# Early Q and K loads, and one 64-column selection turn for chunks 1 to 3, in a fused windowed-attention and maxout-FFN kernel

## The chip, the cores and the metric

The kernel runs on one core of one Trainium2 chip. The metric is device time in microseconds (us), from start to end of one execution. Kernels that were run together ran on the same chip and shared runs of the kernel before. A ratio is the mean time of one kernel's fast runs over that of the other's of the same rounds, with a 95% interval, so it isn't quite the ratio of the medians that are quoted beside it. Four runs count as slow (one of e4, three of the kernel before in sets B and C); the ratios leave them out, the quoted medians and ranges hold them. The experiments ran in three sets on three chips (set A: e1, e2, e4, e5; set B: e6, e8, e9, e10; set C: e3, e11, e12, e13). Between sets I compare ratios to the kernel before, not times.

## The reference, cut to what matters

```python
# attention: q, k, v are (4, 8, 768, 64): 4 batches, 8 heads, 768 tokens, 64 per head
scores = (1 / np.sqrt(D)) * np.matmul(q, k.transpose(0, 1, 3, 2))
keep = (pos[None, :] < 4) | ((rel >= 0) & (rel < 128))        # 4 sink tokens, window of 128
a = softmax(np.where(keep, scores, -1e9))
x = np.matmul(a, v)  # heads side by side: 3072 tokens x 512
# maxout FFN: w1, w2, w3 are 512 x 768, w_out is 768 x 512
h = np.maximum(np.maximum(x @ w1, x @ w2), x @ w3)
out = (h @ w_out).astype(np.float32)
```

## The kernel before

The tokens are worked through in 12 chunks of 256, three to a batch. For each chunk Q and K are loaded and turned (head dimension onto partitions), the scores are made, exponentials taken, multiplied with V ("AV"), the result is turned and goes into the FFN. All instructions are placed by hand: every engine works its own list in order, so an instruction that waits holds up all later ones of its engine (in e12 below a cast starts 5.9 us after its data have landed). In the order string, `K`, `Q` are turns, `B` the mask bias in PSUM, `S` scores, `A` AV, `T` the turn of the result, `F` a group of the FFN; the letter after it names the chunk (`a` is chunk 0, `b` is chunk 1 in the start).

Two kinds of loads exist. Chunk 0 goes through SyncE's queue in fp32 and is cast on VectorE; chunks 1 and 2 go through Pool's queue in runs of 16 tokens and are converted to bf16 by the load:

```python
def load_runs(ci):
    ...
    for j, src in ((0, k), (1, q)):
        nc.gpsimd.dma_start(
            out=runs[ci][:, j],
            in_=src[b, :, t0:t0 + 256].rearrange("h (r x) d -> h r (x d)", x=16))
```

Runs are turned by matmuls with columns of the identity. Chunk 1 uses 64 columns of the data at a time; chunk 2 uses 128, which takes half as many matmuls but leaves each head's data on the wrong half of the partitions for half of it, so that the copies out of PSUM are 64 partitions by 256:

```python
def prep_runs(ci, j, g):
    ...
    if ci == 1:
        for i in range(2):
            pt = psum.tile([128, 8, NP, 16], F32, tag="f", name="pt")
            for u in range(8):
                for h in range(2):
                    nc.tensor.matmul(pt[64 * h:64 * h + 64, u],
                                     lhsT=x[:, 128 * u + 64 * i:128 * u + 64 * i + 64],
                                     rhs=heads[:, h], start=True, stop=True)
            ...                                    # one wide copy out, L258 or L260
        return
    pt = psum.tile([128, 8, 4, 16], F32, tag="f", name="pt")
    for u in range(8):
        nc.tensor.matmul(pt[:, u], lhsT=x[:, 128 * u:128 * u + 128],
                         rhs=ident[:, 64 * g:64 * g + 64], start=True, stop=True)   # L264
    ...                                            # four narrow copies out, L271 or L273
```

Chunk 3 is loaded in fp32 and cast on Pool. The start:

```python
load(0)                                  # SyncE queue: K, Q, K, Q of chunk 0, then its V
...                                      # Pool: identity, four selects, masks, sel, v_sink
sink_v_init()
load_runs(1)                             # Pool queue, its first loads
load_v(1, nc.gpsimd)
load_w(0, 0, 256)
load_w(0, 256, d_ff)
warm(36)                                 # filler matmuls that keep TensorE's clock up
...
run("Ka1 Sa01 Qa1 Ba23", a=0)
run("Sa23", a=0)
cast_v(0, 0, nc.vector)
cast_v(0, 1, nc.vector)
nc.gpsimd.tensor_copy(v_sink[:, :, 0:D], vs_raw)
sink_k(0, nc.gpsimd.tensor_copy)
load_w(1, 0, 256)
load_w(1, 256, d_ff)
load_w(2)
...
warm(3)
run("Aa0 Aa1 Aa2 Aa3 Kb0 Qb0 Ta0 Ta1 Bb01 Sb01 Zb", a=0, b=1)
```

The softmax here doesn't subtract the row's maximum and nothing guards it: scores larger than these inputs give would overflow.

## Time and profile before

| kernel before | |
|---|---|
| time | 184.04 us median of 3 runs, 182.4 to 184.81 |
| span in the profile | 181.6 us |
| TensorE busy | 94% of the span |
| bytes read, written | 25.2 MB, 6.29 MB |

The prediction below shows the busy row, the chain and the stretches. The page's slices: 40 equal parts of the span, each digit a share in tenths (9 is 90% or more). These are the clock that TensorE was granted, and the busy share of the DMA engines:

```profile
PEclk9999999999999999999999999999999999999999
DMA  4999999899598989991589989898799742132404
```

The clock is at its full rate throughout, and the DMA engines are busy for 80% or more of slices 2 to 10, the first 45 us. The order of time in the first 30 us (start, duration, engine, line, operation, output<-input, shapes, count, and in brackets the idle time before it and what ended it):

```profile
5.55 0.94 POOL L84 DMA_DIRECT2D runs<-in_k_dram  x1
...
6.84 0.51 DVE L203 CAST qk_bf<-qk_raw 128x512 bf16<-128x512 f32 x1 [0.26 <-DMA qk_raw<-in_q_dram]
...
8.61 2.18 DVE L212 CAST ve<-v_raw 64x512 bf16<-64x512 f32 x4 [0.34 <-DMA v_raw<-in_v_dram]
...
10.84 0.80 PE L374 MATMUL o_ps<-ve,e_sb 128*128 128x65 bf16 x21 [0.73 <-DVE ve L212]
...
10.89 2.23 POOL L162 DMA_DIRECT2D w<-in_moe_w_dram  x3
...
13.16 0.70 PE L253 MATMUL pt<-ident,runs 128*64 128x64 bf16 x32 [0.89 <-DMA runs<-in_q_dram]
```

Pool's first load is issued at 5.55 us, and when it begins to move, at 7.38 (see below), nearly all of chunk 0 is in: its last piece of Q is cast at 6.84, its V at 8.61 as it lands, and AV of chunk 0 starts in earnest at 10.84 (three matmuls of it at 9.84), before chunk 1's runs are turned. Below, the start of AV is always that of its main part.

### The profile page before, as it was taken

Reading aid. Unit: us, or ns where it says so; the run is one execution under the profiler, and the core shown is the slowest. Engines: PE = TensorE matmul, PEld = TensorE weight load, DVE = VectorE, ACT = ScalarE, POOL = GpSimd, SP = SyncE. Lnnn points to the kernel's source line nnn. Section 1 sums busy time; section 2 is a strip of 40 time slices with the busy share of each in tenths; the row PEclk is TensorE's granted clock in tenths of the full one; section 3 lists DMA queues with packets and bytes.
Section 4 is the critical chain, followed back from the end, with each engine's and each line's share of the span. In section 5 each row is a group of like instructions: output and inputs, shape, how many; then the busy total and the mean of one; then the engine's idle time right before and its main releaser. Section 6 shows DMA issues by size and latency. Waiting matters only on the chain.

```text
span 181.6 us, 4832 instructions
## 1 busy us (share of the span) xinstructions
PE 170.8 (94%) x1953; PEld 131.6 (72%) x1953; DVE 118.4 (65%) x251; ACT 92.1 (51%) x197; POOL 70.7 (39%) x121
## 2 busy tenths in 40 slices
PE   6949999979999999999999899999999999999991
PEld 6645789755698688588598488687696796796880
DVE  1785435997299189577667767676695785673451
ACT  2537651962881781951933922923826716622220
POOL 7986700657621565565014623626244400000001
PEclk9999999999999999999999999999999999999999
DMA  4999999899598989991589989898799742132404
GB/s 142 236 182 204 209 206 249 191 288 289 144 187 207 255 209 302 228 296 64 105 221 306 161 239 270 152 269 229 159 298 198 135 106 58 34 85 58 119 2 116
DMA packets 64646, 33.64 MB, mean 185 GB/s; under 512 B 26640, under 2 KB 60944, under 8 KB 64624
## 3 DMA queue, kind: packets, MB, share of 16 engines
q1 hardware_dynamic: 59520, 27.70, 64.1%
q0 software_dynamic: 4864, 5.38, 16.4%
q8 instruction: 15, 0.25, 0.6%
q10 hardware_dynamic: 240, 0.26, 0.6%
q14 instruction: 7, 0.06, 0.1%
HBM read 25.20 MB, written 6.29 MB: 173 GB/s over the span
## 4 chain that ended last, share of the span: by engine, by line
PE 76%; DMA 11%; DVE 3%; SPq 2%; ACT 2%; issue 1%; POOL 1%; POOLq 0%
PE h_ps L412 49%; PE y_ps L433 15%; DMA w<-in_moe_w_dram 7%; PE o_ps L374 5%; PE st L322 3%; DMA xT<-x_sb 2%; DMA vs_raw<-in_v_dram 2%; DVE h_sb L418 2%; PE y_ps L452 1%; SPq L70 1%; SPq L110 1%; ACT e_sb L328 1%; DVE kk L273 1%; PE o_ps L361 1%; PE sk L341 1%
## 5 line engine op out<-in xcount | busy, mean ns | idle before, releaser
L412 PE MATMUL h_ps<-xT,w 128*128 128x256 bf16 x864 | 103.5, 273 | 1.2 <-DMA xT<-x_sb 0.6
L412 PEld LDWEIGHTS <-w 128*128 128x128 bf16 x864 | 81.3, 98 | 13.2 <-issue 1.4
L418 DVE TENSOR_TENSOR h_sb<-h_sb,h_ps 128x512 bf16<-128x512 bf16 x72 | 49.1, 684 | 27.0 <-PE h_ps L412 22.3
L328 ACT ACTIVATE e_sb<-st 128x512 bf16<-128x512 f32 (+1 forms) x96 | 45.2, 594 | 5.5 <-PE st L322 5.4
L416 ACT CAST h_sb<-h_ps 128x512 bf16<-128x512 f32 x36 | 21.8, 611 | 46.8 <-PE h_ps L412 46.7
L212 POOL CAST ve<-v_raw 64x512 bf16<-64x512 f32 x44 | 31.2, 709 | 27.3 <-DMA v_raw<-in_v_dram 22.0
L203 POOL CAST qk_bf<-qk_raw 128x512 bf16<-128x512 f32 x36 | 22.8, 635 | 44.5 <-DMA qk_raw<-in_k_dram 27.6
L335 DVE TENSOR_TENSOR e_sb<-e_sb,msk 128x1024 bf16<-128x1024 bf16 (+1 forms) x40 | 29.1, 741 | 16.3 <-ACT e_sb L328 16.1
L433 PE MATMUL y_ps<-wo,h_sb 128*128 128x512 bf16 x132 | 30.7, 379 | 0.3
L433 PEld LDWEIGHTS <-h_sb 128*128 128x128 bf16 x132 | 12.4, 97 | 14.0 <-issue 1.1
L382 DVE TENSOR_TENSOR x_sb<-o_ps,rc 128x256 bf16<-128x256 f32 x48 | 20.4, 425 | 1.7
L374 PE MATMUL o_ps<-ve,e_sb 128*128 128x65 bf16 x352 | 17.8, 193 | 1.4 <-DVE ve L212 1.4
L374 PEld LDWEIGHTS <-e_sb 128*128 128x128 bf16 x352 | 15.7, 97 | 3.5 <-DVE ve L212 0.9
L439 ACT COPY y_sb<-y_ps 128x512 f32<-128x512 f32 x22 | 12.6, 632 | 10.9 <-PE y_ps L433 10.7
L322 PE MATMUL st<-qT,kk 64*128 64x128 bf16 (+1 forms) x256 | 13.5, 237 | 0.5 <-ACT qT L236 0.3
L423 POOL DMA_DIRECT2D out_dram<-y_sb x1 | 0.6, 573 | 34.1 <-ACT y_sb L463 34.1
L322 PEld LDWEIGHTS <-kk 64*128 64x128 bf16 x256 | 8.8, 94 | 4.7 <-issue 2.5
L379 DVE RECIPROCAL rc<-o_ps 128x4 f32<-128x4 f32 x48 | 8.4, 176 | 5.3 <-PE o_ps L374 5.2
L346 ACT ACTIVATE e_sink<-sk 128x256 bf16<-128x256 f32 x8 | 3.2, 394 | 5.6 <-PE sk L341 5.6
L128 PE MATMUL warm<-ident 128*128 128x128 bf16 x43 | 4.3, 282 | 1.4 <-POOL ident masks.py:199 1.4
L399 ACT COPY xT<-xt_ps 128x512 bf16<-128x512 bf16 x8 | 4.3, 593 | 2.1 <-PE xt_ps L397 2.1
L128 PEld LDWEIGHTS <-ident 128*128 128x128 bf16 x43 | 3.9, 134 | 1.6 <-POOL ident masks.py:199 1.4
(62 smaller groups left out, 77.9 us busy)
## 6 DMA issues: line engine op xcount, KB each, us to landing
out_dram<-y_sb SPq DMA_DIRECT2D x22, 256.0 KB, 5.1
qk_raw<-in_k_dram SPq DMA_DIRECT2D x20, 256.0 KB, 4.1
qk_raw<-in_q_dram SPq DMA_DIRECT2D x20, 256.0 KB, 4.4
v_raw<-in_v_dram SPq DMA_DIRECT2D x10, 512.0 KB, 7.1
v_raw<-in_v_dram POOLq DMA_DIRECT2D x2, 512.0 KB, 10.5
w<-in_moe_w_dram POOLq DMA_DIRECT2D x2, 512.0 KB, 11.9
w<-in_moe_w_dram POOLq DMA_DIRECT2D x1, 768.0 KB, 15.4
wo<-in_moe_w_out_dram POOLq DMA_DIRECT2D x2, 384.0 KB, 14.4
```

Of the source, the lines that this page charges most:

```text
L203: (eng.tensor_copy if eng else nc.scalar.copy)(dst.rearrange("p i (h d) -> p h i d", d=D), src)
L212: (eng.tensor_copy if eng else nc.scalar.copy)(dst[64 * i:64 * i + 64], src[64 * n:64 * n + 64, :, i])
L322: nc.tensor.matmul(st[h][:, sl], lhsT=kx[r, p, k0:k0 + 128], rhs=qx[r], start=ci >= 2, stop=True, skip_group_check=ci < 2)
L328: nc.scalar.activation(e[:, h, lo:], st[:, lo:], AF.Exp, scale=scale)
L335: nc.vector.tensor_tensor(out=e, in0=e, in1=m, op=ALU.mult)
L374: nc.tensor.matmul(o[:, t, h], lhsT=es[ci, p][:, h, sl], rhs=ve[b % 2][:, n, 2 * p + h], start=(c == 0 and x == 0), stop=(x == len(blocks) ...
L382: nc.vector.tensor_mul(xs[ci][:, :, 2 * p:2 * p + 2], o[:, :, :, 0:D], rc.unsqueeze(3).to_broadcast([128, 2, 2, D]))
L412: nc.tensor.matmul(hp[:, f], lhsT=w_sb[wi, 2 * fp + f][:, ds], rhs=xTs[ci][:, :, ds], start=(ds == 0), stop=(ds == DS - 1))
L416: nc.scalar.copy(dst, hp)
L418: nc.vector.tensor_max(dst, dst, hp)
L433: nc.tensor.matmul(yps[ci, t], lhsT=hs[ci][:, fb, t * 128:(t + 1) * 128], rhs=wo[:, fb], start=(fb == 0), stop=(fb == FB - 1))
L439: nc.scalar.copy(y[:, t], yps.pop((ci, t)))
```

## The change

The intent: Pool is busy with masks before it can issue its first load, so cut that work to two selects and let VectorE do the rest while it is idle; load chunk 1's runs right after those selects; give chunk 2 the same 64-column turn with wide copies as chunk 1; give chunk 3 runs too, so that it needs no casts; and turn chunk 1's K before, and its Q just before, the AV of chunk 0.

```diff
-        nc.gpsimd.memset(msk[:, 0:2], 1.0)
+        nc.gpsimd.memset(msk[:, 1], 1.0)
         for i in range(2):
-            for slot, op, sign in ((1, ALU.is_ge, 1), (0, ALU.is_gt, -1)):
-                ...                                   # four selects on Pool
+            ...                                       # two selects on Pool
+        load_runs(1)
+        nc.vector.tensor_scalar(out=msk[:, 0], in0=msk[:, 1], scalar1=-1.0, scalar2=1.0, ...)
+        ...               # mask copies, bias terms, sel, v_sink: all on VectorE
 ...
-        def prep_runs(ci, j, g):                      # 64 columns for chunk 1, 128 for chunk 2
+        def prep(ci, j):                              # 64 columns, wide copies, chunks 1 to 3
 ...
-        sink_v_init()
-        load_runs(1)
         load_v(1, nc.gpsimd)
         load_w(0, 0, 256)
         load_w(0, 256, d_ff)
 ...
-        run("Ka1 Sa01 Qa1 Ba23", a=0)
-        run("Sa23", a=0)
+        run("Ka1 Sa01 Qa1 Ba23 Sa23 Kb", a=0, b=1)
         cast_v(0, 0, nc.vector)
-        cast_v(0, 1, nc.vector)
+        cast_v(0, 1, nc.gpsimd)
 ...
-        warm(3)
-        run("Aa0 Aa1 Aa2 Aa3 Kb0 Qb0 Ta0 Ta1 Bb01 Sb01 Zb", a=0, b=1)
+        load_runs(3)
+        warm(24)
+        run("Qb Aa0 Aa1 Aa2 Aa3 Bb01 Sb01 Zb", a=0, b=1)
         sink_v()
-        run("Bb23 Sb23 Fa0 Vb ...")
+        run("Bb23 Ta0 Ta1 Sb23 Fa0 Vb ...")
 ...
-        load(3, nc.gpsimd)
+        load_v(3, nc.gpsimd)
-        run("... Kc0 Qc0 Fa2 Kc1 Qc1 Fa5 Sc01 ...")
+        run("... Kc Fa2 Qc Fa5 Sc01 ...")
 ...
-        run("Ac2 Ac3 Yb0 Tc0 Tc1 Kd0 Qd0 Yb1 Kd1 Qd1", b=1, c=2, d=3)
+        run("Ac2 Ac3 Kd Yb0 Qd Tc0 Tc1 Yb1", b=1, c=2, d=3)
```

## The prediction

> **What bounds the kernel now.** I read the busy row and the slices of the page first, then the chain of work that ended last, then the order of time from 0 to 50 us, the waits of TensorE, and the time to landing of each load.
>
> ```profile
> PE 170.8 (94%) x1953; PEld 131.6 (72%) x1953; DVE 118.4 (65%) x251; ACT 92.1 (51%) x197; POOL 70.7 (39%) x121
> ...
> PE 76%; DMA 11%; DVE 3%; SPq 2%; ACT 2%; issue 1%; POOL 1%; POOLq 0%
> ```
>
> TensorE carries 76% of the chain; the second term is DMA. So I ask where TensorE is late before it becomes saturated. Busy time by stretches (the columns are us, then busy of PE, PEld, DVE, ACT, POOL, clock, DMA share, GB/s):
>
> ```profile
> 5.00:10.00 5.00, 4.21 (x52) 2.61 (x49) 4.17 (x11) 3.29 (x9) 5.00 (x11) 1.00 0.93 216
> 10.00:15.00 5.00, 3.37 (x100) 2.61 (x97) 4.49 (x14) 1.54 (x4) 3.08 (x8) 1.00 1.01 198
> ...
> 35.00:40.00 5.00, 3.90 (x52) 2.66 (x50) 4.94 (x9) 4.16 (x9) 2.40 (x6) 1.00 1.00 289
> ...
> 50.00:60.00 10.00, 10.00 (x108) 8.33 (x107) 8.95 (x19) 4.66 (x14) 2.69 (x4) 1.00 1.15 207
> ```
>
> Before 50 us TensorE idles 5.7 us (50 minus the 44.3 us that all stretches before 50 us add up to); from 50 us on it is nearly full, about 1.2 us of idle up to 170 us, and the tail is untouched by the change. So only the first 50 us can give much. The chain there:
>
> ```profile
> 11.63 12.39 DMA w<-in_moe_w_dram
> 24.02 0.05 issue
> 24.07 7.16 PE h_ps L412 x64
> ...
> 34.32 0.41 DVE kk L273
> ...
> 36.07 0.69 DVE h_sb L418
> 36.76 0.17 DVE e_sb L335
> 36.93 0.72 issue
> 37.65 0.68 DVE e_sb L335
> 38.33 1.20 DVE h_sb L418 x2
> ```
>
> The reader is to see two places. Up to 24.02 us the chain is a weight load, and TensorE waited for it only 0.2 us: the load and TensorE's own work arrive together. From 34 to 39.5 us it is VectorE, held by eight small copies of K of chunk 2 (L273); 1.1 us of TensorE's idle time hangs on it (the wait of L361 for DVE h_sb).
>
> The landings (issue plus time to landing, asked one load at a time): runs of chunk 1, K 11.25 and Q 13.1 us; first weight pieces 16.5 and 20.05; second 21.5 and 24.0; third 27.75; runs of chunk 2 28.5 and 30.6; its V 32.0; output weights 33.7 and 35.65. The first FFN group on each piece starts at 17.84, 20.16, about 22.4 and 24.07 us. TensorE trails the weight queue by 0 to 1.3 us all the way.
>
> **What the Trainium skill says.** "DMA: Bandwidth & Descriptors", Specifications, gives about 358 GB/s as the HBM limit of one core. The trace agrees: from about 9 us to 35.65 us the Pool queue reads 9.43 MB in fp32 (K and Q of two chunks 2.10, V of two chunks 1.05, four weights 6.29), or 355 GB/s, though the page shows some 200 GB/s, as it counts the bf16 that is written. The same section puts the first byte of a Pool load at about 1 us. The trace differs: the first such load is issued at 5.55 us, yet the 1.6 MB moved up to 8 us is just what the SyncE queue carries, and from 8 to 9 us only 85 GB/s move. So about 3 us passed. "VectorE: DVE Perf Modes", Mode 1×, names PSUM operands as the case of one result per cycle. It agrees: 256 elements took 420 ns (L273), 512 took 681 (L260), 1.02 ns for each further element and some 160 ns fixed, so few wide copies beat many narrow ones. "TensorE: Matmul & The Clock Gate", LDWEIGHTS, says that a load costs by its columns. The trace agrees in part: 32 turns of 64 columns took 0.69 us (L253) and 16 of 128 columns 0.63 us (L264).
>
> **The change, part by part.**
>
> 1. Pool start. Removed from Pool before its first load: two of four selects (2 × 0.29), the copies of the masks (0.40 + 0.50), two memsets (0.83), the `sel` and `v_sink` work (0.30 + 0.38 + 0.42), and half a memset (0.1): 3.5 us. The runs of chunk 1 are then issued at about 2.1 us in place of 5.55. VectorE takes the mask work while it waits for its first data (idle from 1.2 to 3.9 us): about ten small instructions of 0.1 to 0.3 us. It is hidden, or delays the first cast by a few tenths.
>
> 2. Turn of chunk 1. K now turns before the values of chunk 0 are used, Q just after 24 filler matmuls (36 took 3.62 us, so 2.4 us). This removes TensorE's wait for Q (0.9 us at 12.3 to 13.2) and takes the copies of 1.28 us (VectorE) and 1.07 us (ACT) off the way to the scores. V of chunk 0 is cast half on VectorE and half on Pool. But the early Pool traffic now meets the SyncE loads of chunk 0 from about 5 us, and V of chunk 0 lands perhaps 1 to 2 us later than 8.6. I expect the scores of chunk 1 at 13.5 to 14.7 us, not 15.2: 0.5 to 1.7 us earlier.
>
> 3. Weights. The gain of part 2 counts only as far as the weights come earlier, since TensorE meets them at 20.05 and 24.0. The bytes ahead of them are the same. What can be filled is the weak stretch: DMA shares of 0.53, 0.84, 0.99 and 0.86 from 8 to 12 us and 0.67 and 0.79 at 2 to 3 and 4 to 5 us. Their shortfalls add to 0.78 and 0.54 us. I take **1.0 us** of the 1.3. The second weight's issue slips, as Pool first casts half of V (2 × 0.62): from 10.9 to perhaps 12 or 13 us; the queue still holds the first weight until about 19, so this costs nothing.
>
> 4. Chunk 2. Eight copies of 420 ns (3.36 us) become two of 681 (1.36): VectorE gains **2.0 us** exactly where it is full (4.94 of 5). ACT's eight of 367 ns (2.94) become two of 588 (1.18). The 1.1 us of TensorE idle should go: **−1.1 us**. TensorE pays: 64 narrow matmuls for 32 wide. In the chain 16 wide cost 0.47; 32 narrow, less the 0.11 us of a last matmul's tail, cost 0.58. Twice 0.11 is **+0.2 us**.
>
> 5. Chunk 3. No casts on Pool (4 × 0.63 = 2.5 us, off the path), 64 narrow matmuls (1.16 us) for 16 transposes (2 × 0.45): **+0.3 us**. The wait of the scores for ACT's qT (0.3 us at 48.9) should go: **−0.3**. Its loads come as 4 KB reads in one-half the written bytes, which lightens the DMA, off the path.
>
> 6. Chunks 4 and later: same work. The layout of the cast changes nothing in size. **0**.
>
> Sum: −1.0 − 1.1 + 0.2 + 0.3 − 0.3 = −1.9 us, so 184.0 − 1.9 = **182.1 us**.
>
> **The rivals.**
>
> *The weights hide the whole start.* If the queue is bound by HBM reads and not by its late start, the second weight still lands at 24.0 and TensorE merely waits for it, where it was busy before. For: TensorE trails the weights so closely; 355 GB/s is at the limit. Against: the weak stretch from 8 to 12 us is real. Then only parts 4 and 5 remain, −0.9: 183.1 us.
>
> *The new traffic starves chunk 0.* The Pool queue's packets took 98 ns each on average and SyncE's 31 (16.4% of the span for 4864 packets, 64.1% for 59520), so a shared engine would give Pool the greater part, and K and Q of chunk 0 come late, at the head of everything. For: this share. Against: only the last quarters are still to come at 5 us, and the chain has about 1 us of slack to the first weight piece. If the start were delayed by 1 us and not gained: about 183.5 to 184.
>
> *VectorE stays the bound at 35 to 40 us for other reasons* (masks of 770 ns and maxima of 684 ns; ACT's exponentials feed it). For: after the copies are gone it is still some 9.5 us busy of 11.5. Against: its backlog begins with L273. Then −0.4 of the 1.1: 182.8 us.
>
> *All of the early slack is real.* If the weights come 2 to 2.5 us earlier, since reads fill HBM from 3 us on: 180.6 to 181 us.
>
> **Range and chances.** The middle case gives 182.1. The rivals span 180.6 to 184, and the medians of before already spread from 182.4 to 184.8. For faster by over 2% the time would have to fall below 180.4, which needs every favourable case at once. I give 8 in 10 to **180.3 to 183.8**; faster by over 2% 0.1, within 2% 0.87, slower 0.03.
>
> **What the profile after would show.** Part 1: the first runs issued near 2.1 us. Part 2: no wait of pt for runs; scores of chunk 1 before 14.7 us. Part 3: the second weight's last piece lands near 23 us; if it lands at 24 with TensorE waiting some 1 us for it, the first rival holds. Part 4: two kk copies near 0.68 us each for chunk 2, TensorE idle from 35 to 40 us under 0.3 us. Part 5: no wait for qT before the scores of chunk 3. The stretches after 50 us should keep their lengths. The prediction is wrong if chunk 0's loads slip by over 2 us, if TensorE cools during a longer wait (the clock row shows less than 9), or if the late stage, full on TensorE before, grows a new wait for a transposed tile.

## The result, and the profile after

| | before | changed |
|---|---|---|
| median of 4 runs each, us | 183.86 (182.4 to 184.81) | 191.03 (190.3 to 192.11) |
| span in the profile, us | 181.6 | 190.4 |
| mean granted clock | 1.0 | 0.973 |
| ratio | | 1.0402, 95% 1.0313 to 1.0491 |

The changed kernel is 4% slower; the prediction had said about 1% faster, and its whole range missed. (The profiled run of the changed kernel took 192.11 us, its slowest, so the span is about 1 us above what is typical.)

The page of the changed kernel: the busy row, the same two rows of slices as shown of before, and the chain by engine.

```profile
PE 176.0 (92%) x2042; PEld 135.3 (71%) x2054; DVE 116.3 (61%) x251; ACT 90.3 (47%) x191; POOL 67.6 (36%) x112
...
PEclk9955999999999999999999999999999999999999
...
DMA  5998199999949999997289999489699942042403
...
PE 74%; DMA 11%; ACT 4%; DVE 4%; issue 3%; SPq 2%; ACTq 0%
```

Two things are new, both in the first 25 us: a stretch at half clock, in slices 3 and 4, and a slice (the fifth, 19 to 24 us) in which the DMA engines hardly work. The stretches say the same with numbers (columns as in the prediction):

```profile
5.00:10.00 5.00, 2.17 (x21) 1.39 (x18) 1.48 (x6) 0.59 (x1) 1.21 (x2) 0.95 1.02 203
10.00:15.00 5.00, 2.86 (x20) 1.58 (x20) 1.46 (x4) 1.64 (x4) 0.00 (x0) 0.50 1.19 231
```

From 5 to 10 us TensorE was busy 4.21 us of 5 before, and is 2.17 now; from 10 to 15 it ran 20 matmuls where it had run 100. The DMA engines are full in both (1.02 and 1.19), so bytes do move: the question is which. The order of time in the first 30 us, the lines that answer to those of before:

```profile
2.18 0.77 POOL L82 DMA_DIRECT2D runs<-in_k_dram  x1
...
9.85 0.43 DVE L194 CAST qk_bf<-qk_raw 128x512 bf16<-128x512 f32 x1 [3.14 <-DMA qk_raw<-in_k_dram]
...
13.02 0.43 DVE L194 CAST qk_bf<-qk_raw 128x512 bf16<-128x512 f32 x1 [2.74 <-DMA qk_raw<-in_q_dram]
...
18.49 1.18 DVE L203 CAST ve<-v_raw 64x512 bf16<-64x512 f32 x2 [0.44 <-DMA v_raw<-in_v_dram]
18.52 1.62 POOL L203 CAST ve<-v_raw 64x512 bf16<-64x512 f32 x2 [12.30 <-DMA v_raw<-in_v_dram]
...
20.38 0.91 PE L351 MATMUL o_ps<-ve,e_sb 128*128 128x65 bf16 x24
...
21.15 2.22 POOL L157 DMA_DIRECT2D w<-in_moe_w_dram  x3
```

Pool's loads now begin at 2.18 us, 3.4 us earlier, as intended. But the last pieces of chunk 0's K and Q are cast at 9.85 and 13.02, and its V at 18.49, **9.9 us later than before**. VectorE's brackets name the loads on SyncE's queue as what it waited for. The trace also records every DMA packet with its queue, size and duration. Counted from these, of the 231 GB/s that moved from 10 to 15 us SyncE's queue had 65 and Pool's 166. From 5.5 to 18 us there are 1,587 packets of SyncE's queue, of 0.50 KB and 36 ns on average, and 1,393 of Pool's, of 1.30 KB and 112 ns (those of 4 bytes left out): nearly as many of one as of the other, and Pool's are the longer ones. Before Pool's first packet, at 4.47 us, 0.66 MB of the 1.61 MB that SyncE's queue has for chunk 0 had moved; in the kernel before that packet came at 7.38 us, after 1.50 MB. The runs of chunk 1, which were loaded early, landed at 11.4 (K) and 11.8 us (Q), against 11.3 and 13.1 before: little was gained. Pool's own wait of 12.30 us for V also holds up its next weight loads, which are behind it in its list: 21.15 us in place of 10.89. The chain of work that ended last, over the start:

```profile
2.42 10.58 DMA qk_raw<-in_q_dram
...
13.02 0.44 DVE qk_bf L194
...
17.14 2.67 PE warm L123 x24
...
20.44 0.84 PE o_ps L351 x24
...
31.79 6.27 PE h_ps L389 x56
```

The chain's first 13 us are one load of chunk 0 on SyncE's queue. (The fillers at 17.14 stand in a wait for V: when they end, V is just being cast.) The last line is seven of the eight FFN groups whose row began at 24.07 us before, on a chain through the weight load at 11.63; the first of the eight begins at 30.69 now, 6.6 us later. The first FFN group of chunk 2 starts at 56.32 in place of 49.67 us, 6.65 later, and the end is 8.8 later. So three-quarters of the loss are there before chunk 2's FFN. The rest, some 2 us, comes after it; waits for turned results on TensorE, "DMA xT", grew there from 0.6 to 1.7 us in this profile (see part 6 below).

### The profile page after: what moved, and what is told of

Same layout as the page of the kernel before. It is cut to its first block, busy times and chain, and to the rows that moved or that the text cites. A ratio compares the mean times of both kernels' runs of the same rounds, so it can differ in the third digit from the quotient of the medians.

```text
span 190.4 us, 5008 instructions
## 1 busy us (share of the span) xinstructions
PE 176.0 (92%) x2042; PEld 135.3 (71%) x2054; DVE 116.3 (61%) x251; ACT 90.3 (47%) x191; POOL 67.6 (36%) x112
## 4 chain that ended last, share of the span: by engine, by line
PE 74%; DMA 11%; ACT 4%; DVE 4%; issue 3%; SPq 2%; ACTq 0%
PE h_ps L389 43%; PE y_ps L410 12%; DMA qk_raw<-in_q_dram 6%; PE o_ps L351 6%; DMA xT<-x_sb 5%; ACT e_sb L305 3%; PE st L299 3%; DVE h_sb L395 2%; PE pt L236 2%; PE st L281 2%; PE y_ps L429 1%; PE warm L123 1%; PE xt_ps L374 1%; PE o_ps L338 1%; SPq L68 1%
## 5 line engine op out<-in xcount | busy, mean ns | idle before, releaser
L203 POOL CAST ve<-v_raw 64x512 bf16<-64x512 f32 x46 | 31.9, 693 | 35.7 <-DMA v_raw<-in_v_dram 24.7
L312 DVE TENSOR_TENSOR e_sb<-e_sb,msk 128x1024 bf16<-128x1024 bf16 (+1 forms) x40 | 27.4, 685 | 21.5 <-ACT e_sb L305 21.1
L194 POOL CAST qk_bf<-qk_raw 128x512 bf16<-128x512 f32 x32 | 20.4, 644 | 47.0 <-DMA qk_raw<-in_k_dram 41.8
L410 PE MATMUL y_ps<-wo,h_sb 128*128 128x512 bf16 x120 | 29.9, 379 | 0.9
L359 DVE TENSOR_TENSOR x_sb<-o_ps,rc 128x256 bf16<-128x256 f32 x48 | 20.4, 424 | 1.6
L299 PE MATMUL st<-qT,kk 64*128 64x128 bf16 (+1 forms) x256 | 14.1, 244 | 0.5 <-DVE h_sb L395 0.2
L123 PE MATMUL warm<-ident 128*128 128x128 bf16 x64 | 7.2, 308 | 1.4 <-POOL ident masks.py:199 1.4
L123 PEld LDWEIGHTS <-ident 128*128 128x128 bf16 x64 | 6.6, 147 | 1.5 <-POOL ident masks.py:199 1.4
L241 ACT CAST qT<-pt 128x512 bf16<-128x512 f32 x6 | 3.2, 592 | 7.6 <-PE pt L236 7.6
L217 PE MATMUL pt<-ident,qk_bf 128*128 128x128 bf16 x16 | 2.2, 285 | 5.0 <-DVE qk_bf L194 5.0
```

Source lines behind the costliest of these rows:

```text
L123: nc.tensor.matmul(wp, lhsT=ident, rhs=ident, start=True, stop=True)
L194: (eng.tensor_copy if eng else nc.scalar.copy)(dst.rearrange("p i (h d) -> p h i d", d=D), src)
L203: (eng.tensor_copy if eng else nc.scalar.copy)(dst[64 * i:64 * i + 64], src[64 * n:64 * n + 64, :, i])
L299: nc.tensor.matmul(st[h][:, sl], lhsT=kx[r, p, k0:k0 + 128], rhs=qx[r], start=ci >= 2, stop=True, skip_group_check=ci < 2)
L312: nc.vector.tensor_tensor(out=e, in0=e, in1=m, op=ALU.mult)
L359: nc.vector.tensor_mul(xs[ci][:, :, 2 * p:2 * p + 2], o[:, :, :, 0:D], rc.unsqueeze(3).to_broadcast([128, 2, 2, D]))
```

## The experiments

The first theory, after the result: Pool's early traffic takes DMA capacity from chunk 0's last loads, which are first in the chain (the collision; C, where the texts use letters, and other letters stand for rivals to it). The rivals: the new order of the start with its 24 fillers stands in the way; the idle time costs only because TensorE's clock falls; or the DMA engines' dry slice at 19 to 24 us delays the weights. They tell apart by what comes back when each suspected cause is taken away by itself. All kernels below gave correct results. The texts were written before each run.

### e2: the mask work alone, on the kernel before (set A)

The mask and `sel` work moved to VectorE and the loads issued at 2.18 us, but the order of the kernel before, and chunks 2 and 3 as before.

```diff
 # against the kernel before
-        nc.gpsimd.memset(msk[:, 0:2], 1.0)
-        ...                                  # four selects, copies on Pool
+        nc.gpsimd.memset(msk[:, 1], 1.0)
+        ...                                  # two selects
+        load_runs(1)
+        ...                                  # the rest of the masks, sel, v_sink on VectorE
-        sink_v_init()
-        load_runs(1)
         load_v(1, nc.gpsimd)
```

> The kernel before with the mask part alone: two selects on Pool, the rest of the masks and the sink selector on VectorE, Pool's loads therefore some 3.4 us earlier; order of work, turns, fillers and casts as before. Theory C: the last cast of Q of chunk 0 near 12 to 13 us, the clock halved for some 10 us, 189 to 192 us. Theory F: the order is that of before, so 183 to 185.

Measured: 193.24 us (192.85 to 193.85), ratio 1.0519 (1.0464 to 1.0573). This part alone makes the kernel slower, by a little more than was expected, and by more than the whole change did (though the intervals overlap). VectorE's casts of chunk 0 in the order of time:

```profile
10.00 0.43 DVE L202 CAST qk_bf<-qk_raw 128x512 bf16<-128x512 f32 x1 [3.30 <-DMA qk_raw<-in_k_dram]
...
12.86 0.43 DVE L202 CAST qk_bf<-qk_raw 128x512 bf16<-128x512 f32 x1 [2.43 <-DMA qk_raw<-in_q_dram]
...
18.38 1.98 DVE L211 CAST ve<-v_raw 64x512 bf16<-64x512 f32 x4 [3.97 <-DMA v_raw<-in_v_dram]
```

The same three waits at the same three times (within 0.2 us) as in the changed kernel, without any of its other parts. AV of chunk 0 starts in earnest at 20.4 us.

### e1: the changed kernel, its Pool loads held back (set A)

```diff
+        scr = const.tile([128, 256], BF16, name="scr")
+        for _ in range(11):
+            nc.gpsimd.memset(scr, 0.0)
         load_runs(1)
```

> The changed kernel with eleven empty memsets on Pool (about 3.4 us) ahead of its first load; nothing else differs, so Pool's first load goes out near 5.5 us as before the change. Theory C (collision: Pool's early loads take the DMA engines from the last quarters of K and Q of chunk 0): the last cast of Q of chunk 0 starts near 6.9 us again instead of 13.0, the clock stays full, the time is 182 to 183.5 us, below the kernel before. Theory F (the new order of the start, 24 fillers, V cast half on Pool): 188 us or more, since all of that is still there. Theory L (the late waits for transposed tiles are the main loss): 186 to 189.

Measured: 188.24 us (187.57 to 188.42), ratio 1.0237 (1.0186 to 1.0288). The first load is issued at 7.16 us. Chunk 0's last Q now lands at 7.6 and its V at 9.2 us, so the collision is gone, and the ratio falls from 1.0402 to 1.0237, some 3 us (it missed what I had expected of the collision alone, 182 to 183.5). But 4 us of loss remain with chunk 0 on time, so starvation can't be all of it. In the profile TensorE waits 3.0 us for the runs of chunk 1 (K lands at 12.7); only after their copy does VectorE cast its half of V, at 14.56, and AV starts at 16.82 us, where it was 10.84 before. That is the second cause: **in the new order the turn of chunk 1's K stands ahead of chunk 0's V in VectorE's and TensorE's lists.** With late loads this could be due to the lateness itself, so it needed e12.

### e12 and e8: the same load time, new and old order (sets C and B)

e12 is the changed kernel with 5 memsets in place of e1's 11; its first load is issued at 4.0 us. e8 is issued at the same time and has the order of the kernel before, with the parts for chunks 2 and 3 and the masks on VectorE kept:

```diff
 # e8 against e12
-        run("Ka1 Sa01 Qa1 Ba23 Sa23 Kb", a=0, b=1)
+        run("Ka1 Sa01 Qa1 Ba23", a=0)
+        run("Sa23", a=0)
         cast_v(0, 0, nc.vector)
-        cast_v(0, 1, nc.gpsimd)
+        cast_v(0, 1, nc.vector)
-        warm(24)
-        run("Qb Aa0 Aa1 Aa2 Aa3 Bb01 Sb01 Zb", a=0, b=1)
+        warm(3)
+        run("Aa0 Aa1 Aa2 Aa3 Kb0 Qb0 Ta0 Ta1 Bb01 Sb01 Zb", a=0, b=1)
-        run("Bb23 Ta0 Ta1 Sb23 Fa0 Vb ...")
+        run("Bb23 Sb23 Fa0 Vb ...")
```

> The changed kernel with five empty memsets ahead of Pool's first load, so near 4.0 us: there the old order gave 183.4 with chunk 0 hardly late (last quarter of Q 7.7, V 10.0) and the runs of K of chunk 1 landing at 13.2 us. Theory two-sided: the new order then waits for those runs at 13 us: 186.5 to 188.5. Theory collision alone: 182.5 to 184, as the collision is gone.

> As the kernel before with the changes for chunks 2 and 3 and with the masks on VectorE, but order of the start as before and five empty memsets (0.45 us each beside VectorE) ahead of Pool's first load, so that it goes out near 4.5 us: between 2.2 (the masks-alone run, 193) and 5.55 (before). Theory C (a matter of how early the Pool queue comes in): the last quarter of Q of chunk 0 lands near 8 us, V of chunk 0 near 10.5, time 183 to 186. If the collision had a threshold and not a slope: 182 to 183 or 190.

Measured: e12 188.51 us (188.28 to 189.3), ratio 1.0316 (1.0272 to 1.0359); e8 183.42 us (182.53 to 183.62), ratio 0.9984 (0.9927 to 1.0041). The intervals are far apart. In e12 chunk 0 isn't late at all: its Q lands at 7.0 and its V at 8.6 us, as early as in the kernel before. Its order of time:

```profile
8.64 1.28 POOL L206 CAST ve<-v_raw 64x512 bf16<-64x512 f32 x2 [0.16 <-DMA v_raw<-in_v_dram]
...
12.85 0.69 PE L239 MATMUL pt<-ident,runs 128*64 128x64 bf16 x32 [2.96 <-DMA runs<-in_k_dram]
...
13.33 1.29 DVE L246 CAST kk<-pt 128x512 bf16<-128x512 f32 x2 [4.08 <-PE pt L239]
...
13.47 2.23 PE L123 MATMUL warm<-ident 128*128 128x128 bf16 x24
...
14.53 1.22 DVE L206 CAST ve<-v_raw 64x512 bf16<-64x512 f32 x2
...
16.63 1.27 PE L354 MATMUL o_ps<-ve,e_sb 128*128 128x65 bf16 x24
```

And AV in e8:

```profile
11.76 0.80 PE L354 MATMUL o_ps<-ve,e_sb 128*128 128x65 bf16 x21 [0.63 <-DVE ve L206]
```

Pool casts its half of V at 8.64, as soon as it lands. VectorE's half is as ready, but VectorE stands at the copy of chunk 1's K for 4.08 us, TensorE stands 2.96 us for that K's runs, and the second half of V is cast at 14.53. AV starts at 16.63 us; in e8 at 11.76. So the new order costs some 3% by itself, 5 to 6 us, when chunk 0 is on time. (e8 also casts both halves of V on VectorE, and ran on another chip; that split wasn't tested alone.)

The order is several things at once, and the chains that ended last tell them apart in part. In both kernels the chain goes through the runs' K, which lands at 12.80 us in e12 and 13.27 in e8. From there to the scores of chunk 1 it takes 5.96 us in e12 (18.76) and 2.84 in e8 (16.11). The 3.1 us more are the 24 fillers, 2.16 us, and AV, 1.20 us, which e8 had done while it waited for K; less 0.25 us for the rest (a slower turn of Q, and the turn of the result, which in e12 comes later). Leaving the fillers out would not give back 2.16 us, as AV must also wait for VectorE's cast of V, which ends at 15.75: by my estimate 0.9 us. No run has the new order with few fillers and chunk 0 on time.

Loading earlier doesn't make the turn fit: the runs' K landed at 12.8 us in e12 with a load at 4.0 us and at 12.7 in e1 with one at 7.2. Only with the load at 2.2 us did it land sooner, at 9.0 to 11.4 in the changed kernel and e2 to e5, and there chunk 0 starves.

### e11: the old order with the loads at 7.0 us (set C)

e8 with 11 memsets in place of 5.

> The late-loads run (188.2 us; Pool's first load at 7.2 us) with one thing put back: the order of the start as before the change (K and Q of chunk 1 turned after the values of chunk 0, 3 fillers, V of chunk 0 cast on VectorE alone). Theory two-sided (the new order makes the values of chunk 0, in the queues of TensorE and VectorE, wait for the runs of K of chunk 1, which land at 12.7 us here): 184 to 185.5 us, a little over before for loads that are 1.6 us later. Theory that the order is harmless and late loads alone cost the 4 us: 187.5 to 189.

Measured: 186.21 us (186.11 to 186.55), ratio 1.0185 (1.0146 to 1.0225); more than was expected. AV starts at 11.68 us, but the runs land at 12.3 and 14.5, TensorE waits 1.4 us for them, and the first FFN group of chunk 2 starts at 51.45 in place of 49.67. Here everything behind the runs in Pool's queue is late. Its interval touches that of e1 (1.0186 to 1.0288), so with late loads the cost of the order isn't separated from that of the loads.

The runs side by side, by the time of the first Pool load. The ratio is to the kernel before of the same rounds; "new" and "old" mean the order of the start.

| first Pool load | order | V of chunk 0 lands | AV of chunk 0 starts | us | ratio |
|---|---|---|---|---|---|
| 2.2 | old (e2) | 18.4 | about 20.4 | 193.24 | 1.0519 |
| 2.2 | new (changed) | 18.5 | 20.38 | 191.03 | 1.0402 |
| 4.0 | old (e8) | 10.0 | 11.76 | 183.42 | 0.9984 |
| 4.0 | new (e12) | 8.6 | 16.63 | 188.51 | 1.0316 |
| 5.55 | old (before) | 8.6 | 10.84 | 183.86 | 1 |
| 7.0 | old (e11) | 8.7 | 11.68 | 186.21 | 1.0185 |
| 7.2 | new (e1) | 9.2 | 16.82 | 188.24 | 1.0237 |

Two causes each push AV of chunk 0 back, and they overlap, as whichever is later counts: at 2.2 us V is later than the turn, and there the new order costs nothing more (its kernel is even below e2, with chunks 2 and 3 different as well). Curing the starvation alone leaves +2.4 to +3.2% (e1, e12), putting back the old order alone +5.2% (e2). No run was made between 2.2 and 4.0 us, so whether it sets in there at once or by degrees isn't known. Pool's first packet came at 4.5 us with a load at 2.2 and at 7.0 with one at 4.0; by then 0.66 and 1.40 MB of the 1.61 MB for chunk 0 had moved.

### e9 and e10: which early bytes starve chunk 0 (set B, one run each)

In e9 only the K half of chunk 1's runs (0.52 MB of fp32, in 4 KB pieces) is issued early, in e10 only chunk 1's V (0.52 MB in 512 B pieces); all else on Pool's queue waits until half of V of chunk 0 is cast. They tell whether long pieces take more of the engines than short ones, or whether the bytes count.

```diff
 # e9 against the changed kernel (e10 does the same with load_v(1) early)
-        load_runs(1)
+        runs[1] = raw.tile([128, 2, 16 * D], BF16, tag="runs", bufs=2, name="runs")
+        nc.gpsimd.dma_start(out=runs[1][:, 0], in_=k[0, :, 256:512].rearrange(...))
 ...
+        cast_v(0, 1, nc.gpsimd)
+        nc.gpsimd.dma_start(out=runs[1][:, 1], in_=q[0, :, 256:512].rearrange(...))
         load_v(1, nc.gpsimd)
 ...
-        cast_v(0, 1, nc.gpsimd)                       # its old place, ahead of the second weight
```

> The changed kernel with only the runs of K of chunk 1 early on Pool (0.52 MB read in 4 KB pieces, written as bf16); the runs of Q, V of chunk 1 and the first weight are issued after Pool has cast its half of V of chunk 0. One look. Theory C: the slip of chunk 0 shrinks with the early bytes: last quarter of Q near 8 to 9 us (13.0 in the changed kernel), V near 10 to 11 us (18.5). The Q of chunk 1 then comes late, so the time need not fall much: 186 to 190.

> The changed kernel with only V of chunk 1 early on Pool (0.52 MB read in 512-byte pieces, no cast); the runs and the first weight after Pool has cast its half of V of chunk 0. One look, against e9 with as many bytes read in large pieces. If the size of Pool's pieces decides the sharing: here SyncE's loads lose less, last quarter of Q near 7.5 us against 8.5 or more in e9. If only the number of bytes ahead decides: the same landing in both within 0.5 us. The time: 188 to 192, as the runs of chunk 1 are late.

Measured: Q of chunk 0 lands at 10.1 us in e9 and 9.8 in e10, its V at 11.6 and 11.3. So the number of early bytes matters (all of them early: 13.0 and 18.5 us). On the size of the pieces the pair says less than it was meant to: in the trace Pool's packets are of 2 KB in e9 and of 4 KB in e10, not of 512 B, and from 5.5 us on about as many ran in each (118 in 3.5 us, 123 in 3.0 us, of 176 and 197 ns). Packets as short as SyncE's 0.5 KB weren't tested. As for time, single runs took 193.75 and 193.35 us, both above what I had expected, since the rest of the runs lands at 17.8 to 19.5 us: neither is a cure.

### e5: the clock kept up (set A)

```diff
         run("Qa0 Ba01", a=0)
+        warm(29)
 ...
-        run("Ka1 Sa01 Qa1 Ba23 Sa23 Kb", a=0, b=1)
+        run("Ka1 Sa01", a=0)
+        warm(20)
+        run("Qa1 Ba23 Sa23 Kb", a=0, b=1)
```

> The changed kernel with 49 more filler matmuls in TensorE's two waits for K and Q of chunk 0, so that it does not idle for 3 us. Theory C with the clock as a follower: loads land as before (last cast of Q near 13.0 us), the granted clock stays full, and the work from 13 to 19 us runs faster: 2 us less than the changed kernel, 188 to 189.5. Theory T (the halved clock is the main cause): 186 or less. If the fillers overrun the waits: no gain.

Measured: 190.38 us (190.14 to 191.87), ratio 1.0379 (1.0304 to 1.0454), not separated from the changed kernel's 1.0402; the 2 us that I had expected didn't come. The fillers did what they were for (granted clock 1.0 from 10 to 20 us, though 0.83 from 20 to 30), Q and V of chunk 0 landed at 12.69 and 18.18 as before, and AV started at 19.88. The half clock follows from the wait; it lies within it and costs too little to be separated here.

### e4: the old number of fillers (set A)

`warm(24)` ahead of AV became `warm(3)`.

> The changed kernel with 3 fillers ahead of the turn of Q of chunk 1 instead of 24. In the changed kernel the 24 take 2.7 us at half clock on the chain. Theory C: landing of Q of chunk 0 unchanged near 13.0 us; but V of chunk 0 lands at 18.5 us only, so at most 1 us comes off: 190 to 191. Theory F (fillers on the chain are a main cause): 2.3 us or more come off, 188.5 or less.

Measured: 191.01 us (189.86 to 192.98), ratio 1.0374 (1.0303 to 1.0444). In the changed kernel, where V is late, the fillers aren't the cause. (The 192.98 is the slow run; the fast ones end at 191.54.) By chance the profiled run, of 190.48 us, had Q at 9.72 and V at 16.44 us, though nothing ahead of them differs from the changed kernel: how long chunk 0 is starved varies by 2 to 3 us from run to run.

### e3: the weights ahead of Pool's wait (set C)

```diff
         cast_v(0, 0, nc.vector)
-        cast_v(0, 1, nc.gpsimd)
-        nc.gpsimd.tensor_copy(v_sink[:, :, 0:D], vs_raw)
-        sink_k(0, nc.gpsimd.tensor_copy)
         load_w(1, 0, 256)
         load_w(1, 256, d_ff)
         load_w(2)
+        cast_v(0, 1, nc.gpsimd)
+        nc.gpsimd.tensor_copy(v_sink[:, :, 0:D], vs_raw)
+        sink_k(0, nc.gpsimd.tensor_copy)
```

> The changed kernel with the second and third weight issued ahead of what waits on Pool for V of chunk 0, so that the DMA engines do not run dry from 18.5 to 23 us. Theory two-sided (chain through K, Q and V of chunk 0, the weights being landed by 27.8 us and wanted at 31.8): within 0.7 us of the changed kernel. Theory D (the dry stretch is a main cause): 2 us or more less. If more Pool bytes in the queue make chunk 0 later still: 1 us more.

Measured: 191.75 us (191.4 to 191.88), ratio 1.0481 (1.0433 to 1.0528). The dry slice of the DMA engines is gone, V still lands at 18.3 us, and nothing is gained. It lands no later either, although Pool's queue now holds three weight pieces more, the last of which lands at 26.0 us. So chunk 0 doesn't wait for Pool's queue to empty; it is slow while it shares the engines with it. The late weights look bad in the profile of the changed kernel, but they aren't what is waited for.

### e6 and e13: the later parts alone (sets B and C, five rounds)

e6 is the kernel before with the parts for chunks 2 and 3 and nothing of the new start; e13 with that for chunk 2 only.

```diff
 # e13 against the kernel before
-            pairs = slice(2 * g, 2 * g + 2) if ci > 1 else slice(0, NP)
+            pairs = slice(2 * g, 2 * g + 2) if ci > 2 else slice(0, NP)
-            if ci == 1:
+            if ci <= 2:
-        run("... Kc0 Qc0 Fa2 Kc1 Qc1 Fa5 ...")
+        run("... Kc0 Fa2 Qc0 Fa5 ...")
 # e6 also has: load_runs(3), load_v(3), cast_v(3, ...), load(4, True), "Kd Yb0 Qd"
```

> The kernel before up to the first FFN groups (masks and sink selector on Pool, Pool's first load near 5.5 us, chunk 1 turned after the values of chunk 0, 3 fillers), with only the parts of the change for chunks 2 and 3: runs and 64 narrow turns with two wide copies each for K and Q, load of chunk 4 moved. The prediction's own terms for these parts: -1.1 +0.2 +0.3 -0.3 = -0.9 us, so 183.0 against 184.0. Theory C+F (all of the loss is in the start): 182.5 to 183.5. Theory L (the late stage loses by the moved loads of chunks 3 and 4): 185 or more.

> The kernel before with chunk 2 alone turned in the new way (64 narrow matmuls, two wide copies each for K and Q); chunk 3 and the start as before. With the terms as measured in the chunks-2-and-3 run (some 0.9 us of idle time gone at 35 to 40 us, about 0.5 us more TensorE work for chunk 2 and as much for chunk 3): 0.4 us less than before, a ratio of 0.996 to 1.0. If the predicted terms held: 0.995. Nothing beyond 1% either way.

Measured: e6 183.70 us (183.24 to 184.39), ratio 1.0006 (0.9955 to 1.0058); e13 183.51 us (182.76 to 185.25), ratio 1.0041 (0.9992 to 1.0089); both a little above what was expected. Neither gains, where the prediction counted 0.9 us for each, which e6's interval just excludes. The stretch from 35 to 40 us of e6 shows that the wait did go: TensorE's idle time there fell from 1.10 to 0.15 us.

```profile
35.00:40.00 5.00, 4.85 (x64) 3.52 (x61) 3.76 (x7) 3.74 (x9) 0.52 (x4) 1.00 1.00 244
```

It was given back just ahead of it. The chain over the turns of chunk 2, in the kernel before:

```profile
31.23 0.47 PE pt L264 x16
31.69 0.87 PE h_ps L412 x8
32.57 0.47 PE pt L264 x16
33.03 0.87 PE h_ps L412 x8
```

And in e6:

```profile
31.31 0.62 PE pt L237 x32
31.93 0.98 PE h_ps L390 x8
32.91 0.62 PE pt L237 x32
33.54 0.98 PE h_ps L390 x8
```

Thirty-two narrow turns took 0.62 us where sixteen wide ones took 0.47, and the FFN group after them 0.98 where it took 0.87. How the chain divides a turn and the group behind it rests on modelled ends, so the sum is the safer figure: 1.60 in place of 1.34 us. Twice 0.15 and twice 0.11 are 0.52 us, not the 0.2 that I had allowed. For chunk 3 the same stretch grew from 4.43 to 4.98 us, 0.55 and not 0.3. The saved waits of 0.95 us at 35 to 40 us and of 0.3 at 48.9 meet 1.07 us of new work, and the first FFN group of chunk 2 starts at 49.56, against 49.67: a gain of 0.1 us.

No kernel of these beats the kernel before: the lowest ratio, that of e8, is 0.9984 with an interval that holds 1.

## Why the prediction was wrong, point by point

1. **Part 1, Pool's start: right in itself.** The first load went out at 2.18 us (2.1 predicted). VectorE's mask work put off its first cast of chunk 0 from 3.89 to 4.97 us, more than "a few tenths"; e8, whose first cast comes at 5.02, is level with the kernel before, so this costs nothing that shows.
2. **Part 2 is the step that failed**, in two of its sentences. "V of chunk 0 lands perhaps 1 to 2 us later than 8.6": it landed at 18.5, 9.9 us later. I saw the collision and took it for a delay at the edge, because "only the last quarters are still to come at 5 us". That left out V: in the kernel before, 0.85 of the 1.61 MB for chunk 0 had not moved at 5.0 us. Nor did I count what it would share the engines with: Pool had two runs, a V and two weight pieces (3.1 MB of fp32) in its queue, all issued by 5.3 us, and from 5.5 to 18 us SyncE's queue moved 63 GB/s beside Pool's 145. e2 shows this part by itself at +5.2%. And "K now turns before the values of chunk 0 are used ... This removes TensorE's wait for Q": the wait for Q was exchanged for a longer one for K, with V's cast behind it. e12 shows this by itself at +3.2%, with the fillers that came with it. The scores of chunk 1 came at 22.08 us, not at 13.5 to 14.7.
3. **Part 3, the weights: the gain of 1.0 us never came**, as TensorE was no longer ahead of them. "From 10.9 to perhaps 12 or 13 us" was 21.15. That this "costs nothing" held by luck: e3, with the weights ahead of that wait, isn't faster.
4. **Part 4, chunk 2: mechanism right, a term mis-sized.** The wait fell by 0.95 us (1.1 predicted), and the cost for TensorE was 0.52 us and not 0.2. I had scaled the turns and left out the slower FFN group behind them.
5. **Part 5, chunk 3: the wait went, the cost was 0.55 and not 0.3 us.** With part 4, e6 is level with the kernel before.
6. **Part 6: zero, not contradicted.** From the first FFN group of chunk 2 to the end the profile of the changed kernel takes 134.1 us and that of before 131.9. The six kernels with the old order take 131.9 to 132.9, and the changed kernel, e1, e3, e9, e10 and e12, all of the new order, 133.9 to 134.8; but e4 and e5, also of the new order with other numbers of fillers, take 132.8 and 131.7. So it may go with the new start, but isn't shown, with one profile each. The waits for "xT" were 1.7 us in the changed kernel, 1.8 in e3, 0.4 in e6 and 0 in e12. The cause is left open: some 2 us of the 8.8 between the two profiles are not explained by a part of the change.

Of the rivals, "the new traffic starves chunk 0" named the first cause, and its size, "delayed by 1 us", was what was wrong. Its argument, that a shared engine gives the queue with the longer packets the greater part, fits the packets counted above: nearly one for one, with Pool's busy 78% of the engines' time from 5.5 to 18 us and SyncE's 28%. It wasn't tested by itself, as Pool's packets were long in e9 and e10 too. None of the rivals named the order of the lists. The prediction's last part did name the signs, "if chunk 0's loads slip by over 2 us", "if TensorE cools during a longer wait" and, as part 6 has it, a longer wait for a transposed tile, and gave them too little weight: slower got 0.03.

One of its readings was wrong as well: that "about 3 us passed" before the first Pool load of the kernel before moved a byte. It took the slow stretch from 8 to 9 us for the start. The packets show the first of Pool's queue at 7.38 us, 1.8 us after the issue began. So the prediction had the two queues meet "from about 5 us"; they met at 4.47.

## What to carry to other kernels

An earlier load isn't a gain if it moves ahead of a load that is needed sooner: before advancing a transfer, list which bytes are still under way on the other queues and who waits for them, and count all that will run beside them, not only its first piece. Moving an instruction up an in-order list moves its wait up too: ask, for each engine, what stands behind it that is already ready. And where a profile shows several oddities at once (low clock, a dry DMA slice, late weights), take each away by itself, as most of them follow from one.

## What the Trainium skill lacked or had wrong

- "DMA: Bandwidth & Descriptors", Queues, rings and completion order, says that each DMA engine takes turns between the queue rows that it has work for, a packet at a time. The trace agrees, as it counts packets: 1,587 of SyncE's queue and 1,393 of Pool's from 5.5 to 18 us. What I didn't find there is what this costs a queue of short packets: SyncE's, of 0.50 KB, moved 63 GB/s beside Pool's of 1.30 KB, where it had moved 296 alone (3 to 7 us of the kernel before).
- The same page, Specifications, gives about 1 us to the first byte of a Pool load. From the end of Pool's issuing instruction to its queue's first packet it took 0.6 us in e1 and 0.9 in the kernel before, but 1.5 in the changed kernel and 2.2 in e12, which issue it earlier. With the load at 4.0 us the first packet came at 7.0, which fits the little harm that it did to chunk 0.
- "TensorE: Matmul & The Clock Gate", Part 1, gives an idle window of about 3.4 us for the fall to half clock. The granted clock did change in steps of 3.41 us here, but the window need not be idle: it fell after stretches in which TensorE was busy for 1.23 (changed kernel, 6.11 to 9.53 us), 1.22 (e12) and 1.43 of 3.41 us (e11), and stayed after 2.0 us (the kernel before, 7.90 to 11.32). The way back agrees: full again at 19.77 us, after a stretch in which it was busy throughout.
- I found no page that counts the cost of short turns for the matmuls behind them: a group of eight FFN matmuls took 0.98 us in the chain behind 32 turns of 64 columns and 0.87 behind 16 of 128, and turn and group together 1.60 in place of 1.34 us.
